# One-step sliding-window attention: TensorE's loop with a turn in front, another cut of the last value load, and a part of wq on ten DMA engines

## Chip, cores and metric

One core of a Trainium2 chip. The metric is device time in microseconds (us) of the whole kernel. A core has TensorE (multiplies), VectorE, ScalarE, GpSimd, SyncE (issues most loads), 16 DMA engines that all its loads and stores share, a working memory of 128 partitions, and 8 accumulation banks that TensorE writes.

## What is computed

One token for each of 32 sequences attends to the last W = 512 places of a cache of 2048, with 32 query heads on 8 key heads (each key head serves 4 query heads), head size 128, everything in bf16:

```
q = (x @ wq) as [32, 32 heads, 128]              # x [32, 512], wq [512, 4096]
s = q . k_cache[:, head // 4, 2048-512:] / sqrt(128)
o = softmax(s) @ v_cache[:, head // 4, 2048-512:]
out = o as [32, 4096] @ wo                       # wo [4096, 512]
```

Some 75.5 MB are read once: 33.5 MB of keys, as much of values, 4.2 MB each of wq and wo.

## The kernel before

The 32 sequences are worked in eight groups of four, "quads" q = 0..7. For a quad, 4 sequences x 8 key heads x 4 blocks of 128 places fill the 128 partitions: K_sb and V_sb hold 128 places x 128 numbers per partition, 4 MB each, in two buffers used in turn (q % 2).

The work of each engine is written out as a string of words, an operation with its quad and a range:

- TensorE: `S q.w` scores of half w (L349 on, 16 multiplies), `E q` turns the probabilities to the layout of the values (L363, 16), `P q.a.b` multiplies the groups a to b of the value places (L374, four multiplies a group, 128 for a whole quad), `F q` folds the four heads of a key head (L386, 4).
- VectorE: `T q.w` transposes half w of the keys (L520), `M` maxima, `N` normalises, `B` spreads the probabilities into block diagonals for P, `C` and `I` pick results out of the banks.
- ScalarE: `X` the exponential, `G` copies what E made, `B`, `C`, `I` as on VectorE, `D` copies what F made to o_sel.

TensorE first does PE_HEAD (L20), the scores and E of quads 0 and 1, written out. Then a loop (L437) of four passes runs two rounds a pass, each round by PE_ROUND (L21): with {0} to {3} standing for q-1 to q+2, it does the scores of quad q+2 in two halves, the values of quad q, the fold of q-1 and E of q+2 between them. Words on quads that don't exist in the last pass are jumped over by six guards (L450). After the loop come F6 and F7 and the output: 128 multiplies with wo in three groups (L457 to L469), inside `single`, a loop of one trip (L218) that begins with a branch hint.

Waiting is done on counters. Each word waits for what `awaited` (L399) lists, each counting as a q + b: the transposes T, the picks C (which free the bank that S writes), the spreads B, the copies D and G, and the loads of V. V's loads count on `sem_v` (the first part of a quad) and `sem_v_end` (the second part); GpSimd adds in advance what a quad loaded in one piece will not bring (L290 to L294).

SyncE issues the loads in the order of LOADS (L34): wq in two halves (L204), then K and V of the quads, V5, V6 and V7 in two halves of 64 places per partition, at last wo in three parts W0, W1, W2 of 16, 12 and 4 rows per partition (L260). A K load waits until the quad two before it is transposed, a V load until P of the quad two before has used the same places, wo until T6 is done, since it lies in K's buffer. wq lies in V's second buffer. SyncE's queue is in order: what stands behind a waiting load waits too. x comes on ScalarE's queue in parts of 2, 6, 10 and 14 rows (L199).

Of the kernel before, what the change touches and what calls it, by code (L numbers as in the profile page):

```python
# [2 lines left out]

# [4 lines left out]
F32 = mybir.dt.float32  # L8
# [8 lines left out]

PE_HEAD = "S0.0 S0.1 S1.0 S1.1 E0 E1"  # L20
PE_ROUND = "S{3}.0 P{1}.0.16 F{0} S{3}.1 P{1}.16.28 E{3} P{1}.28.32"  # L21
PE_TAIL = "F6 F7"
ROUNDS = 8
DVE_OPS = """
# [2 lines left out]
C6.2.4 I7.2.0 I7.3.0 I7.2.1 I7.3.1  # L27
"""
ACT_OPS = """
X0 G0 X1 G1 B0.4.8 B1.4.8 X2 G2 C0.0.4 B2.4.8 D0 X3 G3 C1.0.4 B3.4.8 D1 X4 G4 C2.0.4 B4.4.8 D2 X5  # L30
G5 C3.0.4 B5.4.8 D3 X6 G6 C4.0.4 B6.4.8 D4 X7 G7 C5.0.2 B7.4.8 D5 C6.0.2 I7.0.0 I7.1.0 I7.0.1 I7.1.1 D6 D7
"""

LOADS = """  # L34
K0 K1 V0.0.128 K2 K3 V1.0.128 K4 V2.0.128 K5 V3.0.128 K6 V4.0.128 K7 V5.0.64
V5.64.128 V6.0.64 V6.64.128 V7.0.64 V7.64.128 W0 W1 W2
""".split()

X_PARTS = [(0, 2), (2, 8), (8, 18), (18, 32)]
WOP = [(0, 16), (16, 28), (28, 32)]  # L40


def ops_of(text):
    return [(w[0],) + tuple(int(n) for n in w[1:].split(".")) for w in text.split()]


def bass_standalone__sliding_block_cached__sampling_kernel(
# [21 lines left out]
    NI = 32  # L69
    NG = 4  # L70

    rounds = [PE_ROUND.format(q - 1, q, q + 1, q + 2) for q in range(ROUNDS)]
    real = lambda w: int(w[1:].split(".")[0]) < NQ and w != f"F{NQ - 2}"
    rounds = [" ".join(w for w in r.split() if real(w)) for r in rounds]
    orders = {
        "PE": ops_of(" ".join([PE_HEAD] + rounds + [PE_TAIL])),
        "DVE": ops_of(DVE_OPS), "ACT": ops_of(ACT_OPS),
    }

# [7 lines left out]
            return ("both", "I%d" % op[3]), 1  # L87
        return (eng, op[0]), 1

    ends, total = {}, {("ACT", "D"): 2, ("both", "C"): 4}  # L90
    for eng, ops in orders.items():
        for op in ops:
            kind = op[0]
            key, n = counter(eng, op)
            total[key] = total.get(key, 0) + n
            if kind in "BP":
                for i in range(op[2], op[3]):
                    ends[kind, op[1], i] = key + (total[key],)
            elif kind == "C":
                for i in range(op[2], op[3]):  # L100
                    ends[kind, op[1], i] = key + (4 * op[1] + 8,)
            elif kind != "I":
                ends[op] = key + (total[key],)

# [23 lines left out]
    with ExitStack() as es:  # L128
# [20 lines left out]
        negmax = sb("negmax", [P, NQ], F32)  # L149
        sums = sb("sums", [P, NQ], F32)  # L150
        recip = sb("recip", [P, NQ], F32)
        junk = sb("junk", [P, 4], F32)

        wq_sb = V_sb[1][:, :].rearrange("p (kt n) -> p kt n", kt=DKT)
        wo_sb = K_sb[0][:, :].rearrange("p (i n) -> p i n", i=NI)
# [43 lines left out]
        for b0, b1 in X_PARTS:  # L199
            nc.scalar.dma_start(  # L200
                x_sb[b0:b1, :], x[b0:b1].rearrange("b s d -> b (s d)")
            ).then_inc(sem_x, 16)

        def load_wq(i):  # L204

            nc.sync.dma_start(
                wq_sb[:, 2 * i:2 * i + 2, :].rearrange("p k n -> p (k n)"),
                wq.rearrange("(p k) n -> p k n", k=DKT)[:, 2 * i:2 * i + 2].rearrange("p k n -> p (k n)"),
            ).then_inc(sem_wq[i], 16)

        load_wq(0)
        block = es.enter_context(nc.Block())
# [24 lines left out]
        @block.sync  # L237
        def _(sp):
            wait = Waits(sp)
            load_wq(1)  # L240
            wo_r = wo.rearrange("(p i) n -> p i n", i=NI)
            for op in ops_of(" ".join(LOADS)):
                kind, q = op[0], op[1]
                if kind == "K":
                    if q >= 2:
                        wait([ends["T", q - 2, 1]])
                    sp.dma_start(K_sb[q % 2][:, :], rows(k_cache, q)).then_inc(sem_k[q % 2], 16)
                elif kind == "V":
# [5 lines left out]
                    sp.dma_start(
                        V_sb[q % 2][:, r0 * DH:r1 * DH], rows(v_cache, q, r0, r1)
                    ).then_inc((sem_v_end if r0 else sem_v)[q % 2], 16)
# [12 lines left out]
            sp.wait_ge(sem_out, 16)  # L269

        @block.gpsimd
        def _(pool):
            with single(pool):
                wait = Waits(pool)

                def diag(t, pattern, name):
# [13 lines left out]
                whole = [w for w in ops_of(" ".join(LOADS)) if w[0] == "V" and w[2:] == (0, R)]  # L290
                pool.memset(junk[:, 2:3], 0.0).then_inc(
                    sem_v_end[0], 16 * sum(w[1] % 2 == 0 for w in whole))
                pool.memset(junk[:, 3:4], 0.0).then_inc(
                    sem_v_end[1], 16 * sum(w[1] % 2 for w in whole))  # L294
                pool.memset(C_sb[:, 1], 0.0).then_inc(op_sem["both", "C"], 4)
# [27 lines left out]
        def _(pe):  # L323
# [11 lines left out]
            pe.wait_ge(s["dve_xT"], 1)  # L335
            for kt in range(DKT):
                if kt % 2 == 0:
                    pe.wait_ge(sem_wq[kt // 2], 16)
# [60 lines left out]
            def awaited(op):  # L399

                kind = op[0]
                if kind == "S":
                    yield op_sem["DVE", "T%d" % op[2]], 1, 1
                    if op[2] == 0:
                        yield s["pool_quad"], 1, 1
                        yield op_sem["both", "C"], 4, -4
                elif kind == "E":
                    yield op_sem["DVE", "N"], 1, 1
                elif kind == "P":
                    if op[2] == 0:  # L410
# [2 lines left out]
                        yield op_sem["ACT", "D"], 1, 1  # L413
                        yield op_sem["ACT", "G"], 1, 2
                        yield sem_v[op[1] % 2], 8, 16 - 8 * (op[1] % 2)
                    elif op[2] == 16:
                        yield sem_v_end[op[1] % 2], 8, 16 - 8 * (op[1] % 2)
                elif kind == "F" and op[1] < NQ - 1:
                    yield op_sem["both", "C"], 4, 8

            def do(op, value):
                for sm, a, b in awaited(op):
                    if (v := value(op[1], a, b)) is not None:
                        pe.wait_ge(sm, v)
                run[op[0]](*op[1:]).then_inc(op_sem["PE", op[0]], 1)

            def plain(q, a, b):
                return a * q + b if a * q + b > 0 else None
# [4 lines left out]
            for op in ops_of(PE_HEAD):  # L433
                if op == ("E", 0):
                    pe.wait_ge(s["pool_e"], 5)
                do(op, plain)
            with nc.Fori(0, ROUNDS, 2, engines=[mybir.EngineType.PE]) as turn:  # L437
                held = {}

                def looped(q, a, b):  # L440
                    key = (skipped, a, a * q + b)
                    if key not in held:
                        v = turn * a + (a * q + b)
                        held[key] = pe.snap(v & 7 if key == (False, 1, 3) else v)
                    return held[key]

                for p in range(2):
                    words = PE_ROUND.format(p - 1, p, p + 1, p + 2).split()
                    for skipped, group in groupby(words, lambda w: w[0] in "SE" or p == 1 and w[0] == "F"):
                        with pe.If(turn < NQ - 2) if skipped else nullcontext():  # L450
                            for op in ops_of(" ".join(group)):
                                do(op, looped)
            for op in ops_of(PE_TAIL):
                do(op, plain)
            wait([ends["D", NQ - 1]])
            with single(pe):
                for j, (i0, i1) in enumerate(WOP):  # L457
                    pe.wait_ge(sem_wo[j], 16)

                    last = i1 == NI  # L460
                    for cs in ((0, 1), (2, 3)) if last else ((0, 1, 2, 3),):
                        for i in range(i0, i1):
                            for c in cs:
                                ins = pe.matmul(
                                    Y_ps[32 * c:32 * (c + 1), 0:P],
                                    lhsT=o_sel[:, i, :],
                                    rhs=wo_sb[:, i, c * P:(c + 1) * P],
                                    start=i == 0, stop=i == NI - 1, tile_position=(0, 32 * c),
                                )  # L469
                        if last:  # L470
                            ins.then_inc(s["pe_Y"], 1)
# [179 lines left out]
```

## Time and profile before

| | us |
|---|---|
| three runs | 185.06, 184.97, 184.95 (median 184.97) |
| profiled execution | 184.95 |
| its span on the core | 183.1 |
| mean rate of the loads over the span | 413 GB/s |
| TensorE multiplies, busy | 118.9 |
| VectorE, ScalarE, GpSimd, busy | 102.7, 53.0, 17.5 |
| DMA queue q1 (all large loads), packets' time as share of 16 engines' span | 96.6% |
| landing of W0, W1, W2 (last of 16 engines) | 175.18, 178.87, 180.09 |
| landing of V7's halves | 165.40, 170.28 |

The span is counted from the core's first instruction to its last; 1.85 us lie outside it. "Busy" adds up instructions. A DMA has landed when each of the 16 engines that share it has reported its part, so the slowest engine gives the time. "Releaser" and the arrow in a row name what an engine's idle time ended with. PEclk is the TensorE clock that was granted, 1.00 being full.

### The profile page before, as it was taken

The numbers are of one execution on the slowest core, as the hardware profiler recorded it, in microseconds if no ns is written. First come the engines' busy times: TensorE is split into PE (matmuls) and PEld (weight loads), VectorE is DVE, ScalarE is ACT, GpSimd is POOL, SyncE is SP. The second block draws the span as 40 slices with busy tenths as digits, with TensorE's granted clock in tenths as the row PEclk, the third lists the DMA queues.
The fourth block names the chain that finished last, engine by engine and source line by source line (L and its number), as shares of the span: only waits on it lengthen the run. The fifth ranks groups of instructions, "written<-read, shape, count | busy, mean of one in ns | idle before, by whom it ended". The sixth has DMA issues, their size and how long they took to land.

```text
span 183.1 us, 3778 instructions
## 1 busy us (share of the span) xinstructions
PE 118.9 (65%) x1644; PEld 55.4 (30%) x1644; DVE 102.7 (56%) x103; ACT 53.0 (29%) x100; POOL 17.5 (10%) x55
## 2 busy tenths in 40 slices
PE   0089204446203996896289945994599499999772
PEld 0024001003201353353035402541145154454362
DVE  0030999995339729949921895059905993503031
ACT  3000400010590015624700390028302832812041
POOL 7910050202000020020000100020000000000000
PEclk9999855555855699999859965699589999999998
DMA  6999999899999999899999999999989999999980
GB/s 219 418 465 401 451 458 444 387 429 458 454 401 401 458 454 422 383 451 454 437 401 422 458 444 408 408 458 444 444 372 444 408 451 408 444 415 437 420 363 26
DMA packets 3572, 75.63 MB, mean 413 GB/s; under 512 B 432, under 2 KB 496, under 8 KB 624
## 3 DMA queue, kind: packets, MB, share of 16 engines
q1 hardware_dynamic: 3504, 75.53, 96.6%
q8 instruction: 4, 0.07, 0.1%
q10 hardware_dynamic: 64, 0.03, 0.1%
HBM read 75.53 MB, written 0.03 MB: 413 GB/s over the span
## 4 chain that ended last, share of the span: by engine, by line
DMA 52%; PE 32%; DVE 11%; ACT 1%; SPq 1%; ACTq 1%; issue 1%; DVEq 0%
DMA V_sb<-in_v_cache_dram 26%; PE ps L378 19%; DMA K_sb<-in_wo_dram 12%; DMA K_sb<-in_k_cache_dram 11%; DVE KT_sb L522 7%; PE ps L340 4%; DMA bd<-in_x_dram 4%; PE ps L353 4%; PE ps L390 2%; PE ps L366 2%; DVE QT_sb L514 2%; DVE KT_sb L511 1%; ACT C_sb L599 1%; ACTq L200 1%; SPq L260 1%
## 5 line engine op out<-in xcount | busy, mean ns | idle before, releaser
L378 PE MATMUL ps<-V_sb,bd 32*128 32x512 bf16 x1024 | 66.9, 411 | 9.7 <-DMA V_sb<-in_v_cache_dram 9.6
L522 DVE STREAM_TRANSPOSE KT_sb<-K_sb 128x4096 f32<-128x4096 f32 x16 | 70.1, 4421 | 4.2 <-DMA K_sb<-in_k_cache_dram 4.1
L353 PE MATMUL ps<-KT_sb,QBD 128*32 128x512 bf16 x256 | 22.7, 485 | 38.3 <-DVE KT_sb L522 25.8
L378 PEld LDWEIGHTS ps<-V_sb,bd 32*128 32x128 bf16 x1024 | 27.0, 100 | 47.5 <-issue 18.6
L528 DVE TENSOR_REDUCE maxv<-ps 128x1 f32<-128x512 f32 x8 | 5.5, 687 | 30.1 <-PE ps L353 30.1
L353 PEld LDWEIGHTS ps<-KT_sb,QBD 128*32 128x32 bf16 x256 | 6.1, 107 | 50.6 <-issue 22.4
L594 ACT ACTIVATE bd<-PTc,mask 128x512 bf16<-128x512 bf16 x32 | 20.3, 710 | 0.2
L316 POOL COPY QBD<-QT_sb 32x128 bf16<-32x128 bf16 x32 | 9.2, 287 | 102.7 <-PE ps L353 86.4
L581 ACT ACTIVATE P_f<-ps,negmax 128x512 f32<-128x512 f32 x8 | 5.5, 686 | 39.0 <-DVE negmax L530 39.0
L599 ACT ACTIVATE C_sb<-ps 32x512 f32<-32x512 f32 x24 | 14.1, 587 | 5.9 <-PE ps L378 5.7
L606 ACT ACTIVATE o_sel<-ps 128x128 bf16<-128x128 f32 x8 | 2.2, 277 | 34.1 <-PE ps L390 34.1
L588 ACT ACTIVATE PTc<-ps 128x512 bf16<-128x512 f32 x8 | 4.8, 597 | 20.9 <-PE ps L366 20.9
L390 PE MATMUL ps<-C_sb,F_sb 128*128 128x128 f32 x72 | 10.6, 290 | 0.2 <-DVE C_sb L551 0.2
L366 PE MATMUL ps<-P_bf,E_sb 128*128 128x128 bf16 x128 | 9.1, 228 | 2.1 <-DVE P_bf L536 2.1
L390 PEld LDWEIGHTS ps<-C_sb,F_sb 128*128 128x128 f32 x72 | 8.8, 191 | 3.9 <-issue 3.4
L340 PE MATMUL ps<-V_sb,bd 128*128 128x512 bf16 x32 | 9.3, 462 | 0.8 <-DVE bd L490 0.8
L366 PEld LDWEIGHTS ps<-P_bf,E_sb 128*128 128x128 bf16 x128 | 7.7, 102 | 5.6 <-DVE P_bf L536 4.8
L542 DVE TENSOR_SCALAR bd<-PTc,mask 128x512 bf16<-128x512 bf16 x32 | 8.9, 343 | 0.0
L547 DVE COPY C_sb<-ps 32x512 f32<-32x512 f32 x4 | 2.8, 693 | 8.1 <-PE ps L378 8.1
L328 PE MATMUL ps<-bd 32*128 32x128 bf16 x4 | 0.6, 296 | 9.0 <-DMA bd<-in_x_dram 9.0
L511 DVE CAST KT_sb<-ps 128x512 bf16<-128x512 f32 x4 | 2.5, 684 | 6.7 <-PE ps L340 6.7
L575 ACT ACTIVATE KT_sb<-ps 128x512 bf16<-128x512 f32 x4 | 2.1, 603 | 14.3 <-PE ps L340 14.3
(34 smaller groups left out, 36.6 us busy)
## 6 DMA issues: line engine op xcount, KB each, us to landing
K_sb<-in_k_cache_dram SPq DMA_DIRECT2D x8, 4096.0 KB, 22.7
V_sb<-in_v_cache_dram SPq DMA_DIRECT2D x5, 4096.0 KB, 26.4
V_sb<-in_v_cache_dram SPq DMA_DIRECT2D x6, 2048.0 KB, 18.3
V_sb<-in_wq_dram SPq DMA_DIRECT2D x2, 2048.0 KB, 9.8
K_sb<-in_wo_dram SPq DMA_DIRECT2D x1, 2048.0 KB, 17.6
K_sb<-in_wo_dram SPq DMA_DIRECT2D x1, 1536.0 KB, 20.7
K_sb<-in_wo_dram SPq DMA_DIRECT2D x1, 512.0 KB, 21.4
out_dram<-P_bf SPq DMA_DIRECT2D x1, 32.0 KB, 1.5
```

Source lines behind the costliest of these rows:

```text
L316: pool.tensor_copy(QBD[pr, q % 2].rearrange("p (w t) (h c) -> p w t h c", w=2, h=HKV)[:, :, :, :, 4 * b:4 * b + 4], QT_sb[pr, q].rearrange ...
L340: ins = pe.matmul(ps[:, n], lhsT=xT_sb[:, kt, :], rhs=wq_sb[:, kt, n * 512:(n + 1) * 512], start=kt == 0, stop=kt == DKT - 1, tile_positio ...
L353: ins = pe.matmul(s_bank(q)[32 * c:32 * c + 32, :], lhsT=QBD[:, q % 2, 2 * w + t, c0:c0 + 32], rhs=KT_sb[:, w, :, KB * h:KB * h + KB, t], ...
L366: ins = pe.matmul(e_bank(q)[:, e * R:(e + 1) * R], lhsT=E_sb[:, k, e].rearrange("p m j -> p (m j)"), rhs=P_bf[:, k * R:(k + 1) * R], start ...
L378: ins = pe.matmul(o_banks(q)[:, b, :], lhsT=bd[pr, q % 2, 4 * g:4 * g + 4].rearrange("p r h e -> p (r h e)"), rhs=V_sb[q % 2][pr, 512 * g: ...
L390: ins = pe.matmul(f_bank(q)[:, 0:P], lhsT=F_sb[:, d].rearrange("p h d -> p (h d)"), rhs=C_sb[:, q % 2, :, 32 * d:32 * d + 32], start=d == ...
L522: return dve.transpose(KT_sb[:, w].bitcast(F32).rearrange("p r c t -> p r (c t)"), K_sb[q % 2][:, :].bitcast(F32).rearrange("p (r w c) -> ...
L528: dve.tensor_reduce(maxv[:, q:q + 1], s_bank(q), AX.X, ALU.max).then_inc(s["dve_m"], 1)
L542: ins = dve.tensor_scalar(o, i, m, None, op0=ALU.mult)
L581: return act.activation(P_f32[:, :].rearrange("p (k r) -> p k r", k=KB), s_bank(q).rearrange("p (r k) -> p k r", k=KB), ACTF.Exp, bias=neg ...
L594: ins = act.activation(o, i, ACTF.Copy, scale=m)
L599: ins = act.activation(*pick_args(q, r), ACTF.Copy)
```

## The change

Three things are altered.

The head of TensorE's order goes into the loop, as a turn in front: the loop has five passes, and in the first one the guards let only scores and E through. There are two kinds of rounds now. In even rounds both halves of the scores stand first and E last. In odd ones the values are cut at group 24, and a word H, a wait without work, stands for the second half of V1, V3, V5. Eleven guards instead of six, `keys` on in passes one to four, `values` in two to five, `fold` in two to four. The counter of C starts 8 higher. The one-trip loop around the output is gone.

V7 is loaded as 96 and 32 places instead of 64 and 64; P7.0.16 waits for the 96. ScalarE does C0, C2, C4 ahead of G2, G4, G6, and X4, X6 ahead of D1, D3.

wq's second half (16 KB in each of 128 partitions) is loaded as 12 KB in 128 partitions, and the last 4 KB in parts of 48, 40 and 40 partitions. The parts of 40 go to the ten lowest DMA engines.

```diff
-PE_HEAD = "S0.0 S0.1 S1.0 S1.1 E0 E1"
-PE_ROUND = "S{3}.0 P{1}.0.16 F{0} S{3}.1 P{1}.16.28 E{3} P{1}.28.32"
+PE_ROUNDS = (
+    "S{3}.0 S{3}.1 P{1}.0.16 F{0} P{1}.16.32 E{3}",
+    "S{3}.0 P{1}.0.16 F{0} S{3}.1 H{1} P{1}.16.24 P{1}.24.28 E{3} P{1}.28.32",
+)
...
-V5.64.128 V6.0.64 V6.64.128 V7.0.64 V7.64.128 W0 W1 W2
+V5.64.128 V6.0.64 V6.64.128 V7.0.96 V7.96.128 W0 W1 W2
...
+WQ_PARTS = [
+    [(0, 128, 0, 8192)],
+    [(0, 128, 0, 6144), (0, 48, 6144, 8192), (48, 88, 6144, 8192), (88, 128, 6144, 8192)],
+]
...
+        wq_r = wq.rearrange("(p k) n -> p (k n)", k=DKT)
+        wq_f = wq_sb.rearrange("p k n -> p (k n)")
+
         def load_wq(i):
-
-            nc.sync.dma_start(
-                wq_sb[:, 2 * i:2 * i + 2, :].rearrange("p k n -> p (k n)"),
-                wq.rearrange("(p k) n -> p k n", k=DKT)[:, 2 * i:2 * i + 2].rearrange("p k n -> p (k n)"),
-            ).then_inc(sem_wq[i], 16)
+            half = DKT // 2 * HD
+            for p0, p1, c0, c1 in WQ_PARTS[i]:
+                cols = slice(i * half + c0, i * half + c1)
+                nc.sync.dma_start(wq_f[p0:p1, cols], wq_r[p0:p1, cols]).then_inc(sem_wq[i], 16)
...
+        def v_sem(q, r0):
+
+            if r0 == R // 2 and q % 2:
+                return sem_v_half
+            return (sem_v_end if r0 else sem_v)[q % 2]
...
-                    elif op[2] == 16:
+                    elif op[2] == 16 + 8 * (op[1] % 2):
                         yield sem_v_end[op[1] % 2], 8, 16 - 8 * (op[1] % 2)
+                elif kind == "H":
+                    yield sem_v_half, 8, 8
...
-            with nc.Fori(0, ROUNDS, 2, engines=[mybir.EngineType.PE]) as turn:
+            with nc.Fori(0, ROUNDS + 2, 2, engines=[mybir.EngineType.PE]) as turn:
+
+                late = pe.snap((turn + 14) & 15)
...
+                        runs = {"keys": turn < NQ, "values": late < NQ, "fold": late < NQ - 2}
+                        with pe.If(runs[group]):
...
-            with single(pe):
-                for j, (i0, i1) in enumerate(WOP):
-                    pe.wait_ge(sem_wo[j], 16)
+            for j, (i0, i1) in enumerate(WOP):
+                pe.wait_ge(sem_wo[j], 16)
```

More of the change, by code (lines that the diff above doesn't have):

```diff
@@ L1 @@
-from contextlib import ExitStack, nullcontext
+from contextlib import ExitStack
 from itertools import groupby
@@ L29 @@
 ACT_OPS = """
-X0 G0 X1 G1 B0.4.8 B1.4.8 X2 G2 C0.0.4 B2.4.8 D0 X3 G3 C1.0.4 B3.4.8 D1 X4 G4 C2.0.4 B4.4.8 D2 X5
-G5 C3.0.4 B5.4.8 D3 X6 G6 C4.0.4 B6.4.8 D4 X7 G7 C5.0.2 B7.4.8 D5 C6.0.2 I7.0.0 I7.1.0 I7.0.1 I7.1.1 D6 D7
+X0 G0 X1 G1 B0.4.8 B1.4.8 X2 C0.0.4 G2 B2.4.8 D0 X3 G3 C1.0.4 B3.4.8 X4 D1 C2.0.4 G4 B4.4.8 D2 X5
+G5 C3.0.4 B5.4.8 X6 D3 C4.0.4 G6 B6.4.8 D4 X7 G7 C5.0.2 B7.4.8 D5 C6.0.2 I7.0.0 I7.1.0 I7.0.1 I7.1.1 D6 D7
 """
@@ L70, in bass_standalone__sliding_block_cached__sampling_kernel, with round_of @@
     NG = 4
-    rounds = [PE_ROUND.format(q - 1, q, q + 1, q + 2) for q in range(ROUNDS)]
-    real = lambda w: int(w[1:].split(".")[0]) < NQ and w != f"F{NQ - 2}"
-    rounds = [" ".join(w for w in r.split() if real(w)) for r in rounds]
+    def round_of(p, q):
+        return PE_ROUNDS[p].format(q - 1, q, q + 1, q + 2).split()
+    rounds = [[w for w in round_of(q % 2, q) if w[0] != "H"] for q in range(-2, ROUNDS)]
+    real = lambda w: -(w[0] == "F") <= int(w[1:].split(".")[0]) < NQ and w != f"F{NQ - 2}"
+    rounds = [" ".join(w for w in r if real(w)) for r in rounds]
     orders = {
-        "PE": ops_of(" ".join([PE_HEAD] + rounds + [PE_TAIL])),
+        "PE": ops_of(" ".join(rounds + [PE_TAIL])),
         "DVE": ops_of(DVE_OPS), "ACT": ops_of(ACT_OPS),
@@ L88, in counter @@
         return (eng, op[0]), 1
-    ends, total = {}, {("ACT", "D"): 2, ("both", "C"): 4}
+    ends, total = {}, {("ACT", "D"): 2, ("both", "C"): 12}
     for eng, ops in orders.items():
@@ L100, in bass_standalone__sliding_block_cached__sampling_kernel @@
                 for i in range(op[2], op[3]):
-                    ends[kind, op[1], i] = key + (4 * op[1] + 8,)
+                    ends[kind, op[1], i] = key + (4 * op[1] + 16,)
             elif kind != "I":
@@ L151, in bass_standalone__sliding_block_cached__sampling_kernel @@
         recip = sb("recip", [P, NQ], F32)
-        junk = sb("junk", [P, 4], F32)
+        junk = sb("junk", [P, 5], F32)
         wq_sb = V_sb[1][:, :].rearrange("p (kt n) -> p kt n", kt=DKT)
@@ L189, in bass_standalone__sliding_block_cached__sampling_kernel @@
         sem_v_end = [sem(f"sem_v_end{i}") for i in range(2)]
+        sem_v_half = sem("sem_v_half")
         sem_wo = [sem(f"sem_wo{i}") for i in range(len(WOP))]
@@ L255, in _ @@
                         V_sb[q % 2][:, r0 * DH:r1 * DH], rows(v_cache, q, r0, r1)
-                    ).then_inc((sem_v_end if r0 else sem_v)[q % 2], 16)
+                    ).then_inc(v_sem(q, r0), 16)
                 else:
@@ L289, in _ @@
                 pool.memset(F_sb[:, :, :, :], 0.0).then_inc(s["pool_fz"], 1)
[L290 to L295, printed above, removed]
+                loads = [w for w in ops_of(" ".join(LOADS)) if w[0] == "V"]
+                for i, sm in enumerate((sem_v_end[0], sem_v_end[1], sem_v_half)):
+                    quads = (range(0, NQ, 2), range(1, NQ, 2), range(1, NQ - 2, 2))[i]
+                    given = sum(w[1] in quads and v_sem(*w[1:3]) is sm for w in loads)
+                    pool.memset(junk[:, 2 + i:3 + i], 0.0).then_inc(sm, 16 * (len(quads) - given))
+                pool.memset(C_sb[:, 1], 0.0).then_inc(op_sem["both", "C"], 12)
                 diag(E_id[:, :, :].rearrange("p e (b h) -> p e b h", b=4),
@@ L337, in _ @@
                 if kt % 2 == 0:
-                    pe.wait_ge(sem_wq[kt // 2], 16)
+                    pe.wait_ge(sem_wq[kt // 2], 16 * len(WQ_PARTS[kt // 2]))
                 for n in range(8):
@@ L405, in awaited @@
                         yield s["pool_quad"], 1, 1
-                        yield op_sem["both", "C"], 4, -4
+                        yield op_sem["both", "C"], 4, 4
                 elif kind == "E":
@@ L415, in awaited @@
                         yield sem_v[op[1] % 2], 8, 16 - 8 * (op[1] % 2)
-                    elif op[2] == 16:
+                    elif op[2] == 16 + 8 * (op[1] % 2):
                         yield sem_v_end[op[1] % 2], 8, 16 - 8 * (op[1] % 2)
+                elif kind == "H":
+                    yield sem_v_half, 8, 8
                 elif kind == "F" and op[1] < NQ - 1:
-                    yield op_sem["both", "C"], 4, 8
+                    yield op_sem["both", "C"], 4, 16
             def do(op, value):
@@ L424, in do @@
                         pe.wait_ge(sm, v)
-                run[op[0]](*op[1:]).then_inc(op_sem["PE", op[0]], 1)
+                if op[0] in run:
+                    run[op[0]](*op[1:]).then_inc(op_sem["PE", op[0]], 1)
             def plain(q, a, b):
@@ L432, in _, with group_of, looped @@
             pe.wait_ge(s["dve_c"], 7)
[L433 to L436, printed above, removed]
-            with nc.Fori(0, ROUNDS, 2, engines=[mybir.EngineType.PE]) as turn:
-                held = {}
[L440 to L445, printed above, removed]
-                for p in range(2):
[L448 to L451, printed above, removed]
+            pe.wait_ge(s["pool_e"], 5)
+            with nc.Fori(0, ROUNDS + 2, 2, engines=[mybir.EngineType.PE]) as turn:
+                late = pe.snap((turn + 14) & 15)
+                held = {}
+                def group_of(p, w):
+                    return "keys" if w[0] in "SE" else "fold" if p == 1 and w[0] in "FH" else "values"
+                for p in range(2):
+                    for group, ws in groupby(round_of(p, p), lambda w: group_of(p, w)):
+                        def looped(q, a, b):
+                            key = (group, a, a * q + b)
+                            if key not in held:
+                                if group == "keys":
+                                    v = turn * a + (a * q + b - 2 * a)
+                                else:
+                                    v = late * a + (a * q + b)
+                                held[key] = pe.snap(v & 7 if key == ("values", 1, 3) else v)
+                            return held[key]
+                        runs = {"keys": turn < NQ, "values": late < NQ, "fold": late < NQ - 2}
+                        with pe.If(runs[group]):
+                            for op in ops_of(" ".join(ws)):
                                 do(op, looped)
@@ L455, in _ @@
             wait([ends["D", NQ - 1]])
-            with single(pe):
-                for j, (i0, i1) in enumerate(WOP):
-                    pe.wait_ge(sem_wo[j], 16)
[L460 to L471, printed above, removed]
+            for j, (i0, i1) in enumerate(WOP):
+                pe.wait_ge(sem_wo[j], 16)
+                last = i1 == NI
+                for cs in ((0, 1), (2, 3)) if last else ((0, 1, 2, 3),):
+                    for i in range(i0, i1):
+                        for c in cs:
+                            ins = pe.matmul(
+                                Y_ps[32 * c:32 * (c + 1), 0:P],
+                                lhsT=o_sel[:, i, :],
+                                rhs=wo_sb[:, i, c * P:(c + 1) * P],
+                                start=i == 0, stop=i == NI - 1, tile_position=(0, 32 * c),
+                            )
+                    if last:
+                        ins.then_inc(s["pe_Y"], 1)
         def spread_args(q, h):
```

## The prediction

> **What bounds the kernel now.** I read the DMA row first, then the queues, the chain that ended last, and the trace's single DMA packets. The page's rows:
>
> ```profile
> DMA  6999999899999999899999999999989999999980
> ...
> q1 hardware_dynamic: 3504, 75.53, 96.6%
> q8 instruction: 4, 0.07, 0.1%
> ```
>
> The loads fill the 16 DMA engines from end to end. The few code fetches on q8 look like nothing, but each sits on one engine. The end of the chain of waits, and of the time line:
>
> ```profile
> 156.99 0.53 SPq L254
> ...
> 158.67 21.42 DMA K_sb<-in_wo_dram
> 180.09 0.04 issue
> 180.14 0.42 PE ps L464 x15
> ```
>
> ```profile
> 177.22 1.08 PE L464 MATMUL ps<-K_sb,o_sel 128*32 128x128 bf16 x64 [0.65 <-ACT o_sel L606]
> 178.91 0.68 PEld L464 LDWEIGHTS ps<-K_sb,o_sel 128*32 128x32 bf16 x48 [0.79 <-DMA K_sb<-in_wo_dram]
> ...
> 180.14 0.43 PE L464 MATMUL ps<-K_sb,o_sel 128*32 128x128 bf16 x16 [0.37 <-DMA K_sb<-in_wo_dram]
> ```
>
> TensorE is ready before W1 and W2 land; W2's landing at 180.09 sets the end, and 3.0 us of output follow.
>
> Now the packets. On one engine a packet starts 4 ns before its predecessor ends, so the records can be chained into 16 engines without a gap over 60 ns from 1.76 us until the loads end. x is loaded in parts of 2, 6, 10 and 14 rows, one row to an engine. Six chains take three packets of the last three parts, four take two, four take one and two none: the sets are nested, and I call them engines 0-5, 6-9, 10-13 and 14-15. The chains are told apart to within some 10 ns; where two cross, a name may be wrong inside a class, seldom across.
>
> The four 16 KB fetches start at 47.50, 68.42, 77.77 and 85.47, on four engines: one of 14-15, one of 0-5, two of 6-9. A fetch takes 1.02 to 1.09, the data packet behind it 1.69 to 1.76 instead of 1.22: that engine's next landing is 1.55 late, for good. So twelve engines end W2's data at 177.8 to 178.2 and four at 179.25 to 179.65. **The bound is the slowest engine, not the mean.** Work moved between engines is worth time; work saved on all is not to be had.
>
> **The change, part by part.**
>
> *wq.* Each engine's second half of wq was 8 packets of 16 KB, 8 x 609 ns (613 less 4 of overlap) = 4.87. Now it is 8 of 12 KB (464, as W1's) and 3 of 4 KB (159, as W2's), and 8 more of 4 KB on the ten low engines (the two forty-row loads, four rows to an engine; I take them for the ten that got x's ten-row part): 8 x 460 + 11 x 155 + 3 more semaphore writes at 5 ns = 5.40, so **+0.53** on 0-9; 8 x 460 + 3 x 155 + 5 = 4.15, so **-0.72** on 10-15. SyncE issues three more loads at 0.41 (L206); K0, K1 and V0 are issued 1.2 later, at up to 4.2, behind wq that lasts to 12.7: hidden. If that cover were gone it would cost 1.2.
>
> *Fetches.* Up to the four fetches TensorE had come through about 114, 233, 353 and 468 pairs of load and matmul, one fetch per 118 or so; none follows the loop's first pass. The code to the loop's end falls from 36+96+360 = 492 pairs to 36+360 = 396: 396/118 = 3.4, so **three fetches** instead of four, earlier (about 36 to 52 us), as the first turn jumps over the value code. A fetch less frees one engine, not the last one, unless that is the one.
>
> Where the three fall decides the sum. All on 10-15, different engines: those end at 178.02 - 0.72 + 1.55 = 178.85, the low ones at 178.17 + 0.53 = 178.70: 0.80 under 179.65. One on 0-9: 178.07 + 0.53 + 1.55 = 180.15: **0.50 over**. The trace ties no engine to a block of code for certain. If the engine goes with the order of the fetch, the three are those of 47.50, 68.42 and 77.77, two of them low; if it is arbitrary, all three are high in 6x5x4/(16x15x14) = 4%. A mapping that changes with the code's place could give anything. So I take +0.50, and keep -0.80.
>
> *V7 as 96 and 32 rows.* 64 rows take 4.9 us (V6's and V7's landings), so 96 land 2.45 later than 64 did: 165.40 + 2.45 + 0.50 = 168.35. P7.0.16 used to start at 165.50 and fill the wait for the second half (170.28); 64 pairs take 3.57 with 0.43 of drain, so all 128 in one go take 6.7. P7 would end at 168.42 + 6.7 = 175.1 instead of 173.9. From P7's end to the first output matmul stood 3.3 us (fold, copies); the one-trip loop's three instructions (0.28 from 176.93 to 177.21) go. With 0.93, 0.70 and 0.42 for the three output groups, TensorE ends at 175.1 + 3.03 + 2.05 = 180.2, under W2's 180.59 + 0.05 + 0.42 = 181.06. At full clock it is just hidden.
>
> *The clock.* V6's second half lands at 161.0, P6 ends between 164.6 and 165.3, and then TensorE has nothing for 3.1 to 3.7 us. What such gaps did before:
>
> ```profile
> 103.60:107.00 3.40, 1.28 (x22) 0.45 (x19) 3.40 (x2) 2.63 (x5) 0.00 (x0) 1.00 0.87 376
> 107.00:110.40 3.40, 1.90 (x16) 0.44 (x16) 3.40 (x2) 2.87 (x5) 0.00 (x0) 0.50 1.05 453
> ...
> 113.80:117.20 3.40, 3.40 (x36) 1.41 (x32) 0.00 (x0) 0.00 (x0) 0.00 (x0) 0.50 1.03 443
> 141.10:144.50 3.40, 2.00 (x36) 1.17 (x32) 3.40 (x1) 1.93 (x4) 0.00 (x0) 1.00 1.00 424
> ```
>
> Behind a stretch's length stand TensorE's multiplies, then its weight loads; the third column from the right is the granted clock. After a stretch in which TensorE was busy for 1.28 of 3.40 us (38%) the clock fell to 0.50, and it stayed there until a stretch had been full; with 2.00 (59%) it stayed at 1.00. At 0.50 a pair takes 90 ns (44 pairs from 92.37 to 96.34) instead of 56: 3.4 us at half clock lose 1.3. So a gap that covers 2.1 us of a stretch halves the clock; one of 3.4 does in (3.4 + 3.4 - 2 x 2.1)/3.4 = 76% of the phases of such stretches against the kernel. Then P7 ends at 176.4 and TensorE at 181.5, **+0.9**; two cold stretches +1.7. [...]
>
> *TensorE's order.* In the first turn E0 now stands ahead of S1. E0 waits for N0 until 44.4, so S1 moves from 37.5-43.6 to 46-48, and M1, X1, N1 come 3.5 later; behind them VectorE's next transpose waits for K2 until 53.17 anyway (4.1 of idle at L522): hidden, else up to 1. In even rounds S.1 goes ahead of P.0.16: T4.1 ends at 91.66 and V2 lands at 92.33 (hidden), T6.1 at 131.3 and V4 at 131.2 (P4 about 1 later, but S6.1 no longer stands inside it). ScalarE's order follows. More branches (11 guards for 6, 0.07 to 0.21 each) run ahead of TensorE's queue. None of this matters while loads are queued: SyncE issued each load at least 6.5 us before the work ahead of it ran out (V7's second at 156.99, work until 163.5; V7's first 8.3 ahead). V7's 96 rows wait for 8 groups more of P5, about 1.8: still 6. GpSimd's added memset of one column is at 6 us, off every path.
>
> *Sum.* Profiled execution 184.95 (span 183.1), 0.02 under the median 184.97. 184.95 + 0.50 at full clock, + 0.9 with one cold stretch: three parts cold to one warm gives 0.8, and I take 185.7.
>
> **The rivals.**
>
> 1. *The fetches fall on engines 10-15 only* (or on none). Then W2 lands 0.80 earlier and V7's 96 rows at 166.85; P7 ends at 173.6 warm, TensorE at 178.7, hidden under W2's 179.75: 184.15. Cold: 180.0, so 184.4. For it: the sizes fit, +0.53 against -0.72 + 1.55 = +0.83 on a fetched engine. Against: of the four fetches seen, three were on 0-9. It decides from one fact, no fetch on 0-9. This one ends on the faster side.
> 2. *Warm tail with a low fetch:* the gap ahead of P7 leaves the clock at 1.00 and W2 alone sets the end, 185.45. The rows that saw 59% busy speak for it, the one with 38% against. [...]
> 3. *A cold tail of two stretches, or a late fetch.* Without the one-trip loop and its branch hint, the output code may call for one more block at about 178, on an engine that still has W2 to bring: up to 1.55 more, 186.5. Against: from crossing to fetch stood some 1.5 to 2.4 us, so it would start after the data.
> 4. *The change does nothing to the end:* a cold tail eats a gain of the first rival, or the fetches' lag is absorbed: 184.6 to 185.3.
>
> **How the numbers follow.** Low fetch with a cold tail 0.35 (185.7 to 185.9), low fetch warm 0.11 (185.45), late fetch or two cold stretches 0.06 (186.5), high fetches 0.38 (184.2), nothing 0.10. Rival 1 gets far more than 4% because two orders out of an unknown rule are a thin basis. About 0.2% (0.37 us) is what a measurement can tell from no change. Faster 0.38, within 0.10, slower 0.52. The range takes in both sides, 184.0 to 186.3; the likeliest case alone is 185.4 to 186.2.
>
> **What would show it.** Three instruction packets on q8, before 60 us. In W2's landings, the last engines at about 180.6 (mine) or 179.3 (rival 1), the fetched engine in or out of the ten that take x's ten-row part. In the windows before V7's first landing a gap of 3.5 or more and a granted clock of 0.5 after it, P7's pairs at 90 ns; the output matmuls then wait for o_sel and not for in_wo. My forecast is wrong if W2 lands before 180.0, or if loads run dry anywhere.

## The result and the profile after

| | before | after |
|---|---|---|
| median of 4 executions each, us | 184.96 (184.88 to 185.06) | 188.13 (187.68 to 188.52) |
| ratio, 95% interval | | 1.0163 (1.0135 to 1.0192) |
| profiled execution, span | 184.95, 183.1 | 187.68, 185.8 |
| landing of K0, first and last of 16 engines | 22.44, 22.85 | 23.75, 25.58 |
| landing of W2, first and last | 178.27, 180.09 | 180.44, 182.71 |

The change is slower by 3.2 us, on the side that I gave 0.52, but 1.8 over the upper end of my range. The page after, with the rows that answer to those of before and the row of GB/s under the first:

```profile
DMA  6999999999999999999999999999999999999980
GB/s 212 421 319 353 437 452 452 430 406 409 441 452 434 430 409 423 445 445 437 423 409 430 452 437 437 430 395 445 452 437 388 427 430 437 404 429 411 419 365 19
...
q1 hardware_dynamic: 3668, 75.53, 96.5%
q8 instruction: 4, 0.07, 0.1%
```

The same row of before:

```profile
GB/s 219 418 465 401 451 458 444 387 429 458 454 401 401 458 454 422 383 451 454 437 401 422 458 444 408 408 458 444 444 372 444 408 451 408 444 415 437 420 363 26
```

Read the two rows of GB/s against each other. By the DMA row the engines are busy to nine tenths or more in nearly every slice of both kernels, and the bytes are the same (75.63 MB). But the third and fourth slice (9.3 to 18.6 us) fell from 465 and 401 to 319 and 353. That is where the last part of wq and the first of K0 are loaded. Busy engines moved fewer bytes, so a share of busy time can't show this loss.

The end has the same form as before, 2.6 later. The chain that ended last, of the kernel after:

```profile
162.88 19.84 DMA K_sb<-in_wo_dram
182.71 0.04 issue
182.76 0.42 PE ps L490 x15
```

And TensorE's time line at the end, after:

```profile
166.25 3.63 PE L396 MATMUL ps<-V_sb,bd 32*128 32x512 bf16 x64
170.48 7.08 PE L396 MATMUL ps<-V_sb,bd 32*128 32x512 bf16 x128 [0.60 <-DMA V_sb<-in_v_cache_dram]
...
180.55 1.83 PE L490 MATMUL ps<-K_sb,o_sel 128*32 128x128 bf16 x112 [0.37 <-ACT o_sel L632]
182.76 0.43 PE L490 MATMUL ps<-K_sb,o_sel 128*32 128x128 bf16 x16 [0.38 <-DMA K_sb<-in_wo_dram]
```

P7 (the second row) runs in one go, at full clock, and W2 still lands last. Now the busy time, clock and rate by stretches of 3 us, first before, then after; the last number is GB/s:

```profile
11.00:14.00 3.00, 3.00 (x8) 1.06 (x7) 0.43 (x5) 0.00 (x0) 0.00 (x0) 1.00 1.21 519
14.00:17.00 3.00, 3.00 (x13) 1.28 (x12) 0.00 (x0) 0.00 (x0) 0.00 (x0) 1.00 0.81 350
17.00:20.00 3.00, 2.62 (x13) 0.98 (x10) 1.85 (x4) 1.64 (x4) 0.00 (x0) 1.00 1.22 524
```

```profile
11.00:14.00 3.00, 3.00 (x8) 1.06 (x7) 0.28 (x4) 0.00 (x0) 0.00 (x0) 1.00 1.08 246
14.00:17.00 3.00, 3.00 (x11) 1.25 (x10) 0.00 (x0) 0.00 (x0) 0.00 (x0) 1.00 1.05 348
17.00:20.00 3.00, 3.00 (x15) 1.18 (x12) 1.41 (x3) 1.20 (x3) 0.00 (x0) 1.00 1.07 459
```

One stretch alone can mislead: packets of 32 KB come in step (in the kernel before, the sixteen engines start K0's first within 0.5 us of each other, and a new one every 1.22 us), and a stretch holds two or three rounds of them. Over the three, before has (519 + 350 + 524) / 3 = 464 and after 351. In 9 us that is 1.02 MB less, and at 452 GB/s (the best slices of the kernel after) those bytes take 2.2 us.

The single packets of the trace say the same. After the change, the 128 packets of 12 KB take 460 ns, as I had it. The 128 packets of 4 KB (from 11.0 to 14.7 us) take 291 ns on the mean, 159 to 433. I had priced them at 159 from W2. The 32 KB packets of K0 behind them take up to 2434 ns, where before all took 1213 to 1222; from 16 us on they take 1.22 again. No engine has a gap in this part: the share of busy DMA engines stands at 1.08 and 1.05 from 11 to 17 us.

The landings split the loss in two. My sum said -0.72 on six engines and +0.53 on ten, 1.25 apart. K0 lands in two groups: six engines at 23.75 to 24.36 and ten at 25.09 to 25.58, against 22.44 to 22.85 before. The groups are 1.2 apart, as the sum had it, but both are **2.2 later than the sum** (six by 1.5 instead of -0.7, ten by 2.7 instead of 0.5).

### The profile page after: what moved, and what is told of

It is laid out like the page before. It is cut to its first block, busy times and chain, and to the rows that moved or that the text cites. A ratio compares the mean times of both kernels' runs of the same rounds, so it can differ in the third digit from the quotient of the medians.

```text
span 185.8 us, 3840 instructions
## 1 busy us (share of the span) xinstructions
PE 119.8 (65%) x1644; PEld 56.1 (30%) x1644; DVE 103.0 (55%) x103; ACT 53.2 (29%) x100; POOL 17.5 (9%) x56
## 2 busy tenths in 40 slices
DMA packets 3736, 75.63 MB, mean 407 GB/s; under 512 B 468, under 2 KB 532, under 8 KB 788
## 4 chain that ended last, share of the span: by engine, by line
DMA 65%; DVE 20%; PE 8%; issue 2%; SPq 2%; ACT 0%; DVEq 0%
DMA K_sb<-in_k_cache_dram 54%; DVE KT_sb L548 19%; DMA K_sb<-in_wo_dram 11%; PE ps L396 5%; PE ps L371 2%; SPq L221 1%; PE ps L408 1%; SPq L278 1%; PE ps L384 1%; ACT P_f L607 0%; DVE maxv L554 0%; SPq L272 0%; DVE P_bf L562 0%; DVE P_bf L589 0%; PE ps L490 0%
## 5 line engine op out<-in xcount | busy, mean ns | idle before, releaser
L396 PE MATMUL ps<-V_sb,bd 32*128 32x512 bf16 x1024 | 64.9, 405 | 5.2 <-DMA V_sb<-in_v_cache_dram 4.7
L371 PE MATMUL ps<-KT_sb,QBD 128*32 128x512 bf16 x256 | 23.9, 511 | 35.7 <-DVE KT_sb L548 29.2
L396 PEld LDWEIGHTS ps<-V_sb,bd 32*128 32x128 bf16 x1024 | 26.3, 99 | 41.9 <-issue 14.0
L384 PE MATMUL ps<-P_bf,E_sb 128*128 128x128 bf16 x128 | 10.1, 241 | 11.9 <-DVE P_bf L562 11.9
L384 PEld LDWEIGHTS ps<-P_bf,E_sb 128*128 128x128 bf16 x128 | 8.5, 109 | 15.8 <-DVE P_bf L562 14.5
L358 PE MATMUL ps<-V_sb,bd 128*128 128x512 bf16 x32 | 9.9, 484 | 0.8 <-DVE bd L516 0.8
L601 ACT ACTIVATE KT_sb<-ps 128x512 bf16<-128x512 f32 x4 | 2.1, 602 | 14.7 <-PE ps L358 14.7
```

The costliest lines, as they stand in the source:

```text
L358: ins = pe.matmul(ps[:, n], lhsT=xT_sb[:, kt, :], rhs=wq_sb[:, kt, n * 512:(n + 1) * 512], start=kt == 0, stop=kt == DKT - 1, tile_positio ...
L371: ins = pe.matmul(s_bank(q)[32 * c:32 * c + 32, :], lhsT=QBD[:, q % 2, 2 * w + t, c0:c0 + 32], rhs=KT_sb[:, w, :, KB * h:KB * h + KB, t], ...
L384: ins = pe.matmul(e_bank(q)[:, e * R:(e + 1) * R], lhsT=E_sb[:, k, e].rearrange("p m j -> p (m j)"), rhs=P_bf[:, k * R:(k + 1) * R], start ...
L396: ins = pe.matmul(o_banks(q)[:, b, :], lhsT=bd[pr, q % 2, 4 * g:4 * g + 4].rearrange("p r h e -> p (r h e)"), rhs=V_sb[q % 2][pr, 512 * g: ...
```

## The experiments

The theories named in the expectations:

- **count**: my prediction's sum, packets at the durations of their size, whoever brings them.
- **small pieces**: packets of 4 KB, or more loads, cost more by themselves.
- **ports**: a set of partitions takes in bytes at a limited rate, about what one engine delivers. In a load of 128 partitions each engine has a set of its own. In loads of 48, 40 and 40 partitions the rows go to other engines, two or more meet at one set, and both slow down. This is a supposition: the record of a packet has its size, queue and times, not its partitions.

All times are medians in us. The kernel before, run among the experiments, had medians of 184.93 to 184.99; 5 of its 66 single executions lay at 185.66 to 186.26. The ratio is formed from the executions of both kernels, so where these fall into groups it is not the ratio of the medians.

| kernel | time | ratio to before, 95% interval | K0 lands | W2 lands last |
|---|---|---|---|---|
| wq_only | 187.60 | 1.0136 (1.0119 to 1.0153) | 24.04 to 25.55 | 182.71 |
| wq_4k_128 | 185.03 | 1.0012 (0.9999 to 1.0025) | 22.55 to 23.04 | 180.16 |
| wq_mirror | 187.25 | 1.0129 (1.0112 to 1.0146) | 23.20 to 24.86 | 182.04 |
| wq_48_80 | 186.34 | 1.0072 (1.0055 to 1.0089) | 23.77 to 24.16 | 181.48 |
| wq_64_64 | 190.49 | 1.0295 (1.0280 to 1.0310) | 28.03 to 28.46 | 185.63 |
| wq_2k | 186.32 | 1.0071 (1.0040 to 1.0102) | 23.18 to 24.27 | 181.39 |
| x_match | 187.24 | 1.0084 (1.0047 to 1.0121) | 22.47 to 25.23 | 182.45 |
| x_cross | 189.84 | 1.0233 (1.0189 to 1.0276) | 24.96 to 27.72 | 185.03 |
| loop_v7 | 185.33 | 1.0019 (1.0003 to 1.0036) | 22.45 to 22.93 | 180.10 |
| v7_only | 185.06 | 1.0036 (1.0010 to 1.0061) | 22.56 to 22.89 | 180.20 |
| loop_only | 184.94 | 0.9992 (0.9980 to 1.0004) | 22.41 to 22.79 | 179.95 |
| wq_loop | 187.75 | 1.0139 (1.0115 to 1.0164) | 23.91 to 25.51 | 182.83 |

### Which part: wq's loads alone

`wq_only` is the kernel before with wq's parts as in the change; the loop and V7 stay.

```diff
...
+    [(0, 128, 0, 6144), (0, 48, 6144, 8192), (48, 88, 6144, 8192), (88, 128, 6144, 8192)],
...
```

> The kernel before with the change's wq parts alone (12 KB in 128 partitions, then 4 KB in 48, 40 and 40). Theory count (the sum on record): only the number of packets matters, +0.5 us where a fetch falls on a low engine, 185.5. Theory ports: a load whose rows are not the ones that an engine brings in the big loads makes engines meet at the same places of the working memory, and all slow down: the change's 4 KB packets took 0.23 to 0.43 us and the first 32 KB packets of K0 2.4 instead of 1.2, so +1.9 to +2.7, 187 to 187.7. Theory small pieces (4 KB at a pitch of 32 KB read slowly): the same 187 to 187.7. If this run stays near 185.5, the loop or V7 made the loss.

It came out at 187.60. Its 4 KB packets take 296 ns and K0's up to 2549. wq's parts explain 2.6 of the 3.2 us; count, with +0.5, does not.

### Are small pieces the cost?

`wq_4k_128` has the same 4 KB and the same number of packets, but in one load of 128 partitions.

```diff
+    [(0, 128, 0, 6144), (0, 128, 6144, 8192)],
```

> The kernel before, wq's second half as 12 KB and 4 KB, both in all 128 partitions, so that each engine brings the rows it always brings. Ports and count: 8 x 460 + 8 x 155 ns against 8 x 609, +0.05 us, 185.0, packets of 4 KB at 0.16 us. Small pieces: the 4 KB packets take 0.23 to 0.43, +0.6 to +2, 185.6 to 187.

185.03, no difference. Its 4 KB packets take 161 ns (159 to 172). Small pieces are refuted: neither the size nor one more load costs anything that shows here (1.0012, 0.9999 to 1.0025).

### Does it matter which engines get more?

`wq_mirror` loads the 4 KB in partitions 80 to 128, 0 to 40 and 40 to 80. By the prediction's count of rows, ten engines get the same surplus, but the parts of 40 lie elsewhere. `wq_48_80` takes that surplus away: by the same count 48 partitions are 3 rows for each of 16 engines, 80 are 5, 8 in all, as in one load.

```diff
+    [(0, 128, 0, 6144), (80, 128, 6144, 8192), (0, 40, 6144, 8192), (40, 80, 6144, 8192)],
...
+    [(0, 128, 0, 6144), (0, 48, 6144, 8192), (48, 128, 6144, 8192)],
```

> As wq_only, the same packets for the same engines, but other rows: 4 KB in partitions 80 to 127, then 0 to 39 and 40 to 79. In the 40-row parts the ten engines bring rows near those that they bring in the big loads. Ports: less meeting, +0.5 to +1.5, 185.5 to 186.5, and the packets of the 40-row parts near 0.16 us. Small pieces: as wq_only, 187 to 187.7.

> As wq_only, but the last 80 partitions in one load, five rows to each of 16 engines: no engine gets more bytes, all bring rows that are not theirs. Count: +0.1, 185.1. Ports: all 16 meet, +1 to +2.5, 186 to 187.5. Small pieces: the same as ports here.

In `wq_48_80` the sixteen landings of K0 lie within 0.4 us, so that no surplus shows anywhere, and yet all are about 1.3 late (23.77 to 24.16) and the time is 186.34: count is refuted by this one alone. `wq_mirror` came out at 187.25, above what ports expected (185.5 to 186.5); its 4 KB packets took 258 ns on the mean. Ports had the direction, and I had placed the parts of 40 partitions too favourably.

### How the loss goes with the bytes

`wq_64_64` has no small packet and no surplus: all 16 KB of wq's second half, in two loads of 64 partitions. `wq_2k` has the change's parts with half the bytes.

```diff
+    [(0, 64, 0, 8192), (64, 128, 0, 8192)],
...
+    [(0, 128, 0, 7168), (0, 48, 7168, 8192), (48, 88, 7168, 8192), (88, 128, 7168, 8192)],
```

> The kernel before, with wq's second half (16 KB in each of 128 partitions) in two loads, 64 partitions each, and nothing else changed. Each engine still brings 8 packets of 16 KB, as before: no small packet, no skew, one issue more. Count expects 185.0 and packets of 609 ns. Ports (two engines at a time bring rows for places that in the other loads one engine serves, which halves the rate) expects the 16 KB packets at up to 1.2 us while these two loads last, 8 x 0.61 = up to 4.9 later on every engine: 187.5 to 189.9. A toll that comes once per change of the split, whatever the bytes, expects about what the parts of 48 and 80 gave: 186.3.

> The kernel before with wq's parts as in the change, but the parts of 48, 40 and 40 partitions bring 2 KB of each row instead of 4 KB (the load in front of them 14 KB). Ports expects the loss to go with the bytes: half of the 2.6 that the 4 KB parts cost, 186.2 to 186.5, of which 0.27 is the skew. A toll per load or per change of the split expects 187.3 to 187.6. Count expects 185.25.

`wq_64_64` is the strongest of all: 190.49, from nothing but a load cut in half by partitions. Its stretches from 8 to 17 us:

```profile
8.00:11.00 3.00, 0.59 (x4) 0.35 (x4) 0.01 (x1) 0.00 (x0) 1.66 (x5) 1.00 0.93 191
11.00:14.00 3.00, 2.26 (x6) 0.88 (x7) 1.78 (x8) 0.00 (x0) 0.00 (x0) 1.00 1.08 235
14.00:17.00 3.00, 3.00 (x11) 1.14 (x9) 0.00 (x0) 0.00 (x0) 0.00 (x0) 1.00 0.96 197
```

The mean is 208 GB/s. Before had 437, 519 and 350 there, 435 on the mean. The rate is halved (0.48) while the share of busy DMA engines (the second number from the right) stays at 0.93 to 1.08. The packets of 16 KB take 1249 ns on the mean from 8 us on, against 611 before. K0 lands 5.6 later, and W2 5.5: what is lost here is never made up. `wq_2k` at 186.32 lost 1.4, about half of `wq_only`'s 2.6. Its executions were spread from 185.3 to 187.66, so the half is rough, but a toll per load (187.3 to 187.6) is out: six of the seven lie under it. The loss goes with the bytes.

### Is it the partitions they write to?

So far each odd load differed from the usual ones in the rows that it reads as well as in the partitions that it writes. Two kernels differ in the second alone. Both are the kernel before with four loads more, 8 rows of 16 KB each, into a place that nothing reads. Eight engines bring 4 packets more in either.

```diff
             load_wq(1)
+            spare_kt = KT_sb[:, 1].rearrange("p r c t -> p (r c t)")
+            wq_x = wq.rearrange("(p k) n -> p (k n)", k=DKT)
+            for i in range(4):
+                r = slice(0 + i, 32, 4)      # x_cross: slice(64 + i, 96, 4)
+                sp.dma_start(spare_kt[r, :], wq_x[i:32:4, 0:2 * HD]).then_inc(sem_wq[1], 16)
...
-                    pe.wait_ge(sem_wq[kt // 2], 16)
+                    pe.wait_ge(sem_wq[kt // 2], 16 + 64 * (kt // 2))
```

> The kernel before with four loads more behind wq, 8 rows of 16 KB each (wq's rows 0 to 31 a second time, to a place that nothing reads, KT_sb's second half in partitions 0, 4, 8 to 28, then 1, 5, 9 and so on), so that eight engines bring 4 packets of 16 KB more, each to the partitions that it serves in the loads of 128 partitions. TensorE's projection waits for them. Count and ports agree: packets of about 0.61 us, the eight engines 4 x 0.61 = 2.45 later, the others not at all; the time by the latest engine, 185.9 to 187.5 (as fetches fall).

> The same loads from the same rows by the same engines, but into partitions 64 to 95 (64, 68 to 92 and so on), which in the loads of 128 partitions the other eight engines serve. Count expects exactly the time of the matched ones. Ports expects both groups of engines on the same eight ports: the extra packets at up to 1.22 us instead of 0.61, the eight engines about 4.9 late, and the other eight, which bring nothing more, about 2.45 late because their own packets slow down as well (K0's of 32 KB above 1.8 us while it lasts): 187.5 to 190.

| | x_match | x_cross |
|---|---|---|
| the 32 packets more, mean ns | 612 (611 to 618) | 1145 (729 to 1282) |
| first 32 packets of K0 (32 KB each), mean ns | 1213 (1213 to 1216) | 1946 (1459 to 2544) |
| K0 on the eight engines that bring nothing more | 22.47 to 22.70 | 24.96 to 25.28 |
| K0 on the eight that bring more | 24.88 to 25.23 | 27.48 to 27.72 |

Their stretches, `x_match` first:

```profile
11.00:14.00 3.00, 3.00 (x9) 1.08 (x8) 0.42 (x5) 0.00 (x0) 0.00 (x0) 1.00 1.12 481
14.00:17.00 3.00, 2.91 (x14) 1.19 (x13) 0.00 (x0) 0.00 (x0) 0.00 (x0) 1.00 0.91 393
17.00:20.00 3.00, 2.21 (x11) 0.78 (x8) 2.26 (x4) 2.05 (x4) 0.00 (x0) 1.00 1.22 524
```

```profile
11.00:14.00 3.00, 3.00 (x9) 1.09 (x8) 0.39 (x5) 0.00 (x0) 0.00 (x0) 1.00 1.09 350
14.00:17.00 3.00, 1.59 (x8) 0.51 (x6) 0.00 (x0) 0.00 (x0) 0.00 (x0) 1.00 1.27 306
17.00:20.00 3.00, 1.82 (x9) 0.88 (x10) 0.00 (x0) 0.00 (x0) 0.00 (x0) 1.00 0.94 393
```

The four loads bring the same rows by the same number of engines in the same number of packets. With them going into partitions 0 to 31 all loads together run at 466 GB/s in these 9 us, with them going into 64 to 95 at 350. In `x_match` the surplus costs its own engines 2.4 and the others nothing, so that count (4 x 0.61 = 2.45) holds to a tenth of a microsecond. In `x_cross` it costs its own engines 4.9 and **delays by 2.5 the eight engines that have nothing more to do**. Ports had said 4.9 and 2.45. This settles the cause: where the bytes are written decides (1145 ns a packet for 612). That two engines meet at one set of partitions and get about what one gets is the supposition that forecast these numbers; no trace shows the sets themselves.

The runs don't show which partitions make a set, and they leave the size of the losses open. An estimate from the packets of before: with 64 and 64, eight packets an engine at half the rate are 8 x 0.61 = 4.9 us late; K0 landed 5.6 late. For the change's parts (1.5 late on six engines, 2.7 on ten) and for 48 and 80 (1.3 on all sixteen) no run shows which engines meet where. Why the losses have this size, and why with 48 and 80 all engines land alike, is not shown.

### The loop, V7 and the clock

`loop_v7` is the changed kernel with wq's second half in one load. `loop_only` has V7 in halves as well. `v7_only` is the kernel before with V7 in 96 and 32 rows. `wq_loop` is the changed kernel with V7 in halves. Where V7 is in halves again, the count that GpSimd adds and the guard of H go back with it.

```diff
-    [(0, 128, 0, 6144), (0, 48, 6144, 8192), (48, 88, 6144, 8192), (88, 128, 6144, 8192)],
+    [(0, 128, 0, 8192)],
...
-V5.64.128 V6.0.64 V6.64.128 V7.0.96 V7.96.128 W0 W1 W2
+V5.64.128 V6.0.64 V6.64.128 V7.0.64 V7.64.128 W0 W1 W2
```

> The changed kernel with wq's second half in one load again: the loop with a turn in front, the orders of TensorE and ScalarE, and V7 as 96 and 32 rows. If these cost nothing of their own, three fetches, W2 last at 180.0 to 180.2 behind a fetched engine, 184.9 to 185.2. If the tail pays for V7's cut (P7 cold after a gap, or TensorE behind W2), 185.4 to 185.9 with output multiplies that wait for o_sel. If the fetch that goes was the one that counted, or none falls on an engine that ends late, 183.6 to 184.4.

> The kernel before with V7 in 96 and 32 rows and nothing else. My reasons: P7's first part waits for the 96 rows (167.9 instead of 165.4), its last for the 32; TensorE still ends under W2: 184.9 to 185.2, unless the gap in front of P7 halves the clock, then 185.2 to 185.8, with pairs of P7 at 90 ns.

> The changed kernel with wq's second half in one load and V7 in halves again: what is left are the loop with a turn in front and the orders of TensorE and ScalarE. If my step on them holds, three fetches and W2 last at 180.0 to 180.2 as before, 184.9 to 185.2 in all executions, none at 185.7 to 186.0 (these come from P7's start after the 96 rows, behind a gap). If the loop costs by itself, the runs at 185.7 to 186.0 stay.

`loop_only` gave 184.94, with all eleven executions from 184.74 to 184.98: the loop and the orders cost and bring nothing that shows. `loop_v7` gave two times: six executions at 184.80 to 184.99 and six at 185.67 to 186.00. The profiled one is of the second kind (186.00). Its time line of TensorE, and its clock (third column from the right):

```profile
167.86 8.77 PE L396 MATMUL ps<-V_sb,bd 32*128 32x512 bf16 x128 [2.27 <-DMA V_sb<-in_v_cache_dram]
...
179.61 1.98 PE L490 MATMUL ps<-K_sb,o_sel 128*32 128x128 bf16 x128 [0.37 <-ACT o_sel L632]
```

```profile
165.10:166.80 1.70, 0.49 (x12) 0.00 (x0) 1.14 (x2) 1.15 (x2) 0.00 (x0) 1.00 0.90 376
166.80:168.50 1.70, 0.64 (x12) 0.32 (x16) 0.24 (x1) 0.03 (x1) 0.00 (x0) 1.00 0.97 405
168.50:170.20 1.70, 1.70 (x28) 0.71 (x24) 0.00 (x0) 0.00 (x0) 0.00 (x0) 0.66 1.09 463
170.20:171.90 1.70, 1.70 (x24) 0.64 (x20) 0.00 (x0) 0.00 (x0) 0.00 (x0) 0.50 1.06 453
171.90:173.60 1.70, 1.70 (x32) 0.76 (x28) 0.00 (x0) 0.00 (x0) 0.00 (x0) 0.83 0.95 400
```

This is the prediction's cold tail. TensorE is idle for 2.27 us ahead of P7. From 165.1 to 168.5 it was busy for 0.49 + 0.64 = 1.13 of 3.40 us (33%), and then the clock falls to 0.50, as it did in the kernel before after a stretch of 38%. P7 takes 8.77, where it took 7.08 in the changed kernel. The 128 output multiplies then wait for o_sel and run in one go, though W2 had landed at 180.10. They end at 181.59, 1.0 after W2 would have had them end (180.10 + 0.47). The two kinds of executions lie 0.9 apart, so I take the others for those with a warm tail; no trace of one was made.

`v7_only` falls into two groups as well, but 1.6 apart (eight at 184.91 to 185.36, three at 186.53 to 186.97), and its profiled execution was one of the eight. That one shows something else: the loads ran dry. V7's 96 rows were issued at 157.59 instead of 150.25, since in the old order they wait for the whole word P5.16.28, and twelve engines had ended V6 by 158.5. In the rows of busy time the last number, GB/s, falls:

```profile
158.00:159.60 1.60, 1.52 (x26) 0.70 (x23) 0.02 (x1) 0.62 (x2) 0.00 (x0) 1.00 0.98 292
159.60:161.20 1.60, 1.58 (x32) 0.83 (x36) 1.55 (x3) 1.56 (x3) 0.00 (x0) 1.00 0.78 323
```

Nearly all of this is hidden behind the four engines that were 1.5 late already: W2 lands last at 180.20 instead of 180.09. Whether a later P5 makes the three slow executions is not shown.

> The changed kernel with V7 in halves again, 64 and 64 rows: loop and wq's parts are as in the change. wq's parts alone gave 187.60, the changed kernel 188.13, the loop alone 184.94. If the half microsecond between them comes from V7's cut (P7's start after 96 rows, TensorE close behind W2 or cold), 187.5 to 187.7. If it comes from the loop together with the late keys, 188.0 to 188.3.

187.75 (six executions, 186.42 to 188.02), just above the first expectation. The changed kernel's own executions were 187.68, 187.86, 188.41 and 188.52, and the profiled one is the first. That the two slower ones had a cold P7 would fit `loop_v7`, but no trace shows it: how the last 0.4 us come about stays open.

## Why the prediction was wrong

- **What bounds the kernel: right.** The slowest DMA engine still sets the end. W2's sixteen landings reach from 180.44 to 182.71, and the output tail behind them has its old length (3.0 us).
- **wq's parts: the step that failed.** "8 x 460 + 11 x 155 + 3 more semaphore writes" took the price of a 4 KB packet from W2, a load of 128 partitions, and used it for loads of 48 and 40 partitions. The 460 was right, as were the ten engines and the difference between the groups (1.25 forecast, 1.2 measured). The 155 was 290, and K0's first packets paid as well: a common 2.2 us that the sum didn't have. I gave this step one value instead of bounds, although no row of before showed a load of 48 or 40 partitions next to others. Rate as a property of the places written was a rival I never listed.
- **Fetches: right in number and price; the place came by luck.** Three came during the loads, at 39.41, 50.52 and 56.48 (I had 36 to 52), but not on the engines that the order of the fetches suggested. The landings tell: of the six early engines (33.46 to 34.07 at K1) five are left at V0 (43.18 to 43.78) and four at K2 (52.90 to 53.38), so the first two fetches fell on 10-15 and only the third on 0-9. That one is W2's last landing, 182.71, and one was enough: rival 1 fell, and +0.50 was the right branch, though the order behind it did not hold. The fourth came at 181.65, behind the loads of its engine, as rival 3 had it come, and cost nothing.
- **V7 and TensorE's end: right in kind.** The 96 rows landed at 170.43, 2.1 after the forecast 168.35, with everything else. P7 took 7.0 instead of 6.7, and the output was ready 2.2 us ahead of W2.
- **The clock: the mechanism was right, but it acted at another place in the profiled execution.** After a stretch in which TensorE was busy for 1.63 of 3.40 us (48%), the granted clock of the next was 0.66. P5 begins there, and its first half took 5.19 instead of 3.63:

```profile
144.50:147.90 3.40, 1.63 (x28) 1.00 (x20) 3.40 (x1) 2.66 (x5) 0.00 (x0) 1.00 0.97 414
147.90:151.30 3.40, 3.16 (x37) 1.11 (x40) 3.40 (x2) 2.85 (x5) 0.00 (x0) 0.66 1.03 439
```

The clock itself stood at 0.50 from 148.98 to 152.39, and in the 3.41 us ahead of that TensorE was busy for 1.40 (41%). With K7's landing 2.6 later, this moved P6's end to 169.9 instead of 165, and the gap ahead of P7 shrank to 0.6 (the bracket in the time line above). In `loop_v7`, where the loads come on time, it cost 1.0 (forecast 0.9) in the traced execution, and by their times in 6 of 12 (forecast 76%). A gap of 2.27 us, in 3.40 us that were 33% busy, sufficed there.

- **The order of TensorE: right.** `loop_only` shows 0.9992 (0.9980 to 1.0004).
- **Loads that never run dry: wrong, though it did not set the end.** "8 groups more of P5, about 1.8: still 6" left out that F4 and S7.1 stand between these groups: in `loop_v7` V7's 96 rows were issued at 154.09 instead of 150.25, 3.8 later. In the kernel after P5 was late on top of that, and the issue came at 158.33. The four earliest engines ended V6 at 159.47 to 159.89, waited 0.1 to 0.3 us each, and their first packets of V7 took 1.21 to 1.70 us instead of 0.91. They land V7's rows some 0.5 to 0.8 late; a fifth, whose first two packets took 1.33 and 1.47, is by these delays the last but one to land W2 (182.02). The slowest engine lost nothing: from V6 to V7's rows it took 7.33 us (163.10 to 170.43), in `loop_v7` 7.30. By the prediction's own sign, loads that run dry, this step failed too.
- **A slip without effect:** by the prediction's own terms rival 1 has the 96 rows at 167.05, not 166.85.

With the common 2.2 us put into the sum, W2's slow engines would have been forecast at 180.59 + 2.2 = 182.8; 182.71 was measured. A warm tail then gives 185.45 + 2.2 = 187.65, and the profiled execution had 187.68.

## What to carry to other kernels

Where loads are the bound, ask of each load not only how much every engine brings but into which partitions. In these experiments every cut of wq's second half by partitions made engines late beyond their own bytes (K0 on all sixteen by 1.3 us with 48 and 80, by 5.6 with 64 and 64), and the change paid 2.2 us on all sixteen to free six of them by a forecast 0.72. So keep loads at 128 partitions and cut them by columns, which cost nothing that shows here (`wq_4k_128`: 1.0012). And read GB/s beside the busy share: in `wq_64_64` the engines look as busy (0.93 to 1.08) at half the rate (208 GB/s for 435). When a load is cut elsewhere, ask too which word of the order it now waits for.

## What the runs showed of the hardware

- The place that a load writes to changed its rate: 32 packets of 16 KB from the same rows took 612 ns each into partitions 0 to 31 (`x_match`), 1145 into 64 to 95 (`x_cross`).
- wq's second half, cut into two loads of 64 partitions, ran at about half the rate (208 GB/s for 435, packets of 16 KB in 1249 ns for 611), though all 16 engines took part (`wq_64_64`).
- The delay reached engines that bring nothing more: in `x_cross` they landed K0 at 24.96 to 25.28, in `x_match` at 22.47 to 22.70, 2.5 us for 32 packets of 16 KB.
- After a gap of 2.27 us in TensorE's work its clock fell to 0.50 (some 3.4 us at half in all), and the end came 1.0 us later (`loop_v7`, one trace). After 3.41 us with 41% busy it fell too, to 0.50 for 3.41 us (the kernel after, 148.98 to 152.39).
- Executions of one kernel fell into two groups 0.9 to 1.4 us apart (`loop_v7`: 0.9; `x_match` with two at 185.8 and 185.9 and three at 187.2 to 187.3). In `loop_v7` the one trace of the slower kind shows the tail's clock; in `x_match` the distance (1.4) is about the lag that a fetch leaves (1.55 in the kernel before), but no trace of the quicker kind was made.
